# The branch over a general path: its wait, its hints and its flag, in a fused attention and token-mixing kernel

## The chip, the cores and the metric

The kernel runs on one core of a Trainium2 chip. The metric is the device time of one execution in microseconds (us). Before the change the median of three runs is 108.28 us (108.19 to 108.72). A program of this kind repeats to about 0.5%, or 0.54 us.

A core has five instruction streams that matter here: TensorE (PE; its weight loads are shown as PEld), VectorE (DVE), ScalarE (ACT), GpSimd (POOL) and SyncE (SP). A name with a q, such as DVEq, is the sequencer of that engine, which takes the instructions in program order, carries out waits, register loads and branches itself, and hands the rest to the engine. Stores to DRAM are issued by SP, loads by GpSimd; 16 DMA engines carry them, and they also carry the blocks of instructions that the sequencers ask for (the queues of kind "instruction").

## What is computed

For 4 batches, 8 heads, 768 rows and head size 64: five rounds of Sinkhorn normalisation of an 8x8 matrix for each head, a mix of the 8 blocks of K and V by it, attention within each block of 96 rows, and then a token mixer on the joined heads.

```python
P = sort_net
for _ in range(5):
    P = np.exp(P - np.max(P, axis=-1, keepdims=True))
    P = P / (np.sum(P, axis=-1, keepdims=True) + 1e-09)
    P = P / (np.sum(P, axis=-2, keepdims=True) + 1e-09)
k_sorted = np.einsum('bhij,bhjcd->bhicd', P, k_b)      # v_sorted likewise
scores = scale * np.matmul(q_b, k_sb.transpose(0, 1, 2, 4, 3))
scores = scores - np.max(scores, axis=-1, keepdims=True)
attn = np.exp(scores)
attn = attn / (np.sum(attn, axis=-1, keepdims=True) + 1e-09)
x = np.matmul(attn, v_sb)                              # heads joined: 4 x 768 x 512
W_tok = scale * np.einsum('bsd,btd->bst', x @ w_q, x @ w_k)
out = np.maximum(np.einsum('bst,btd->bsd', W_tok, x), 0.0) @ w_out
```

## The kernel before

The fast path leaves out the maximum of the scores. It takes the plain exponential and keeps the reciprocal of every row sum in `RS`. At the end a test on GpSimd (lines 465 to 472) counts the entries of `RS` that lie between 1e-30 and 1e30, and writes 1 to `bad` if any does not. `bad` is then loaded into a register of four engines (GpSimd, ScalarE, TensorE, VectorE; line 474), and under `tc.If(redo > 0)` (line 476) stands the general path: the whole computation once more, unrolled, with the maximum. With these inputs the flag is 0, and the engines jump over it. Its length is very different from engine to engine: on TensorE it holds thousands of matmuls, on ScalarE the 32 exponentials.

The fast path is unrolled too. The schedule is manual: the string `ORDER` (lines 18 to 51) is the program order, one item for each unit of work, and each engine takes its own items in that order. An item is a letter, the batch, an index, and after the @ a PSUM bank (for TensorE) or the engine. The items that matter here are those of the last batch, 3, at the end of the string:

- `G3.n` builds the small mixing matrix `Ab` from `wk` and `X` (8 matmuls), `g3.0` evacuates it.
- `H3.n` mixes the tokens, 4 matmuls into two banks; `h3.n` is the ReLU into `mixT`, for output rows 2n and 2n+1.
- `O3.n` is one output product (4 matmuls over `mixT` and `wo`; `O3.5` is split into halves a and b), and `o3.n` its evacuation into `ot`, by ScalarE (`@A`) or VectorE (`@D`).
- `y3.n` is the store of one sixth of the last batch, 256 KB, issued by SP (line 445). `ot` has four slots of two sixths each. The six last stores read three of them: slots 1, 2 and 3 hold the sixths 0 and 1, 2 and 3, 4 and 5.
- `P3.n` and `x3.n` are the attention product and its division; `x3.n` writes `RS`, and `x3.1` is the last to do so.

The end of the order before reads:

```python
y2.2@S o3.1@D O3.3@5 o3.0@D O3.4@0 y3.0@S o3.3@A y3.1@S O3.5a@1 y3.3@S o3.4@D O3.5b@7 o3.5a@A O3.2@6
y3.4@S o3.5b@A y3.5@S o3.2@A y3.2@S
```

So the last product is O3.2, the last evacuation o3.2 on ScalarE, and the last store y3.2. Waits follow from the tiles: an instruction that writes a tile waits until the earlier ones that read it are done, a store's landing included.

The branch of line 476 works so on each of the four engines: a first compare-and-branch on the flag, a semaphore instruction that makes up for the counts of the path that is left out, and, with `preferred_fallthrough_block=False`, a second branch to the end of the kernel. There (line 577) each engine runs a drain, SP walks over the semaphores of all queues and engines one by one, and a barrier ends the program.

Of the kernel before, what the change touches and what calls it, by code (L numbers as in the profile page):

```python
# [10 lines left out]
BF16 = mybir.dt.bfloat16  # L11
AX = mybir.AxisListType
ALU = mybir.AluOpType
# [26 lines left out]
P2.2@0 o0.1@A P2.3@4 o0.0@A x2.2@D O0.4@3 P2.0@6 o0.4@A x2.3@D S3.4@0 O0.5@2 e3.4@A x2.0@D H0.1@4  # L40
o0.5@A S3.1@0 T2.3@3 h0.1@A T2.2@2 t2.3@D T2.1@6 T2.0@7 t2.2@D P3.3@4 t2.1@D t2.0@A O0.2@3 x3.3@D
e3.1@A P3.4@6 J2.0@2 o0.2@A x3.4@D P3.0@0 j2.0@A H1.2@4 x3.0@D H1.0@6 W2.0@3 h1.2@A O0.3@2 w2.0@A
P3.2@0 h1.0@A J2.1@3 x3.2@D P3.1@4 j2.1@A O1.0@6 o0.3@A x3.1@D y0.1@S T3.3@7 d2.1@S O1.1@3 y0.2@S
y0.0@S T3.1@2 o1.1@A d2.0@S H1.1@0 t3.1@D W2.1@4 G2.0@5 w2.1@A h1.1@D t3.3@A G2.1@5 T3.0@4 O1.5@7
t3.0@D T3.2@3 o1.5@D O1.4@2 t3.2@A O1.2@4 g2.0@A o1.4@D J3.0@7 o1.0@D O1.3@5 y1.0@S j3.0@D J3.1@0
o1.3@A o1.2@A H2.0@2 j3.1@D W3.0@1 H2.1@6 y1.1@S H2.2@4 w3.0@D W3.1@0 h2.0@D G3.0@1 w3.1@A h2.1@A
G3.1@1 O2.0@0 d3.1@A d3.0@A O2.1@2 o2.0@D O2.3@3 h2.2@D o2.1@A O2.2@0 y2.0@S o2.3@A y1.2@S g3.0@A
O2.5@6 o2.2@A y2.1@S H3.0@4 o2.5@D H3.2@2 H3.1@0 h3.0@A O2.4@7 h3.1@A O3.1@6 o2.4@D h3.2@A O3.0@4
y2.2@S o3.1@D O3.3@5 o3.0@D O3.4@0 y3.0@S o3.3@A y3.1@S O3.5a@1 y3.3@S o3.4@D O3.5b@7 o3.5a@A O3.2@6
y3.4@S o3.5b@A y3.5@S o3.2@A y3.2@S  # L50
"""

UNIT = re.compile(r"([A-Za-z])(\d)\.(\w+?)@(\w)$")
# [3 lines left out]
def kernel(  # L57
# [11 lines left out]
    nc = tc.nc  # L69
    B, H, S, D = q.shape  # L70
    NB = sort_net.shape[-1]
    BLK = S // NB
# [13 lines left out]
    AG = 14  # L86
    NG = -(-NU // AG)
    LAST = B - 1
# [6 lines left out]
    sb = ctx.enter_context(tc.tile_pool(name="sb", bufs=1))  # L95
    psp = ctx.enter_context(tc.tile_pool(name="psp", bufs=1, space=bass.MemoryType.PSUM))

    def tiles(name, n, shape, dtype=BF16):
        return [sb.tile(shape, dtype, name=f"{name}{i}") for i in range(n)]

    PS = psp.tile([P, 8, 512], FP32, name="ps")
# [13 lines left out]
    E = tiles("E", 2, [BLK, NT, EW])  # L115
# [7 lines left out]
    NOT = 4  # L123
    ot = tiles("ot", NOT, [P, 2, DM], FP32)
    M = tiles("M", 2, [P, H, SP, NB])
    RS = sb.tile([BLK, B, NG, 2, AG // 2], FP32, name="RS")
    ok = sb.tile([BLK, B, NG * AG], BF16, name="ok")
# [6 lines left out]
    m_p = sb.tile([P, SP], BF16, name="m_p")  # L134
    gate = sb.tile([1, 1], BF16, name="gate")
    ok1 = sb.tile([1, 1], FP32, name="ok1")
    bad = sb.tile([1, 1], mybir.dt.int32, name="bad")
    fil = sb.tile([P, 512], BF16, name="fil")

# [8 lines left out]
    def mm(o, w, x, start=True, stop=True, t=False):  # L148
        nc.tensor.matmul(o, w, x, is_transpose=t, start=start, stop=stop, skip_group_check=True)  # L149
# [71 lines left out]
    def u_u(b, n, e, bank):  # L221
        copy(e, PTR.rearrange("p i h -> p (i h)"), PS[:, bank, 0:NB * (BH - H)])
# [211 lines left out]
    def oslot(b, n):  # L434
        return ot[(b * 3 + n // 2) % NOT][:, n % 2, :]
# [4 lines left out]
    def u_y(b, n, e):  # L440
# [3 lines left out]
        else:  # L444
            ENG[e].dma_start(out=od[:, n, :], in_=oslot(b, n))

    fns = {kk[2:]: f for kk, f in locals().items() if kk.startswith("u_")}
    halves = {"a": (0, DM // 2), "b": (DM // 2, DM)}
    banks = {}
    fills = dict(u="B", q="Q", k="K", v="V", f="F", e="S", x="P", t="T", j="J", w="W", g="G", h="H", o="O")  # L450
    for item in ORDER.split():
        kind, b, n, arg = UNIT.match(item).groups()
        b, half = int(b), halves.get(n[-1], ())
        num = int(n[:-1] if half else n)
        if kind in "BZQKVFSPTJWGHO":
            banks[kind, b, n] = int(arg)
            fns[kind](b, num, int(arg), *half)
        elif kind in fills:
            fns[kind](b, num, arg, banks[fills[kind], b, "1" if kind in "gu" else n], *half)
        else:  # L460
            fns[kind](b, num, arg)

    okf = ok.rearrange("p b n -> p (b n)")
    rsf = RS.rearrange("p b n a t -> p (b n a t)")
    ok2 = E[1][:, 0, 0:B * NG * AG]
    nc.gpsimd.tensor_scalar(out=okf, in0=rsf, scalar1=1e-30, scalar2=None, op0=ALU.is_ge)  # L468
    nc.gpsimd.tensor_scalar(out=ok2, in0=rsf, scalar1=1e30, scalar2=None, op0=ALU.is_le)
    nc.gpsimd.tensor_tensor(out=okf, in0=okf, in1=ok2, op=ALU.mult)  # L470
    nc.gpsimd.tensor_reduce(out=ok1, in_=okf, op=ALU.add, axis=AX.XYZWC)
    nc.gpsimd.tensor_scalar(out=bad, in0=ok1, scalar1=BLK * B * NG * AG - 0.5, scalar2=None, op0=ALU.is_lt)
    eng = mybir.EngineType
    redo = nc.values_load(bad, engines=(eng.Pool, eng.Activation, eng.PE, eng.DVE), min_val=0, max_val=1)

    with tc.If(redo > 0, preferred_fallthrough_block=False):
        qc = QT[1].rearrange("p k r s -> p k (r s)")
        sx = XT[1][0:BLK].rearrange("p t c -> p (t c)").bitcast(FP32)[:, 0:S]
        ex = E[1][:, 1, 0:S]
        exT = E[1][:, 2, 0:S]  # L480
        mx = RS.rearrange("p b n a t -> p (b n a t)")[:, 0:NB]
        sm = RS.rearrange("p b n a t -> p (b n a t)")[:, NB:2 * NB]

        def bb(t, w):
            return t.unsqueeze(2).to_broadcast([BLK, NB, w])

        spread(0, H, BH)
        u_u(0, 1, "D", 0)
        for b in range(B):
            for n in range(3):  # L490
                nc.gpsimd.dma_start(out=(Qn, Kn, Vn)[n][0].rearrange("p h r d -> p h (r d)"),
                                    in_=(q, k, v)[n][b].rearrange("h (p r) d -> p h (r d)", p=P))
            if b == 0:
                spread(1, 0, H)
                src = PS[:, 1, 0:NB * H].rearrange("p (i h) -> p h i", h=H)
            else:
                src = PTR.rearrange("p i h -> p h i")[:, (b - 1) * H:b * H, :]
            for n in range(NP):
                spread_m("D", 0, n, src)
            for n in range(NP):  # L500
                u_Q(0, n, 2)
                u_q(0, n, "D", 2)
                copy("D", qc[:, n].rearrange("p (i r s) -> p r i s", i=NB, r=R6),
                     QT[0][:, n].rearrange("p r (i s) -> p r i s", i=NB))
                u_K(0, n, 4)
                u_k(0, n, "D", 4)
                sorted_t(Vn, 0, n, 6)
                by_block("D", XT[0][:, n, :], 6)
                u_F(0, n, 3)
                u_f(0, n, "D", 3)  # L510
            for h in range(H):
                kp, o = h // 2, h % 2 * D
                sp = PS[0:BLK, 4:6, 0:4 * BLK].rearrange("p a (i c) -> p a i c", c=BLK)
                for i in range(NB):
                    mm(sp[:, i // 4, i % 4, :], qc[o:o + D, kp, i * BLK:(i + 1) * BLK],
                       KT[0][o:o + D, kp, i * BLK:(i + 1) * BLK])
                copy("D", sx.rearrange("p (a n) -> p a n", a=2), PS[0:BLK, 4:6, 0:4 * BLK])
                s3 = sx.rearrange("p (i c) -> p i c", i=NB)
                nc.vector.reduce_max(mx, s3, axis=AX.X)
                nc.vector.tensor_sub(s3, s3, bb(mx, BLK))  # L520
                nc.scalar.activation(ex, sx, ACT.Exp, scale=scale)
                nc.vector.reduce_sum(sm, ex.rearrange("p (i c) -> p i c", i=NB), axis=AX.X)
                nc.vector.reciprocal(sm, sm)
                for i in range(NB):
                    mm(bf(6)[0:BLK, i * BLK:(i + 1) * BLK], ex[:, i * BLK:(i + 1) * BLK],
                       idb[0:BLK, 0:BLK], t=True)
                copy("D", exT, bf(6)[0:BLK, 0:S])
                op = PS[0:BLK, 7, :].rearrange("p (i d) -> p i d", d=D)
                for i in range(NB):
                    mm(op[:, i, :], exT[:, i * BLK:(i + 1) * BLK], VT[0][:, i, h * D1:h * D1 + D])  # L530
                nc.vector.tensor_mul(X[0][:, kp, :, o:o + D], op, bb(sm, D))
            for n in range(PT):
                u_T(0, n, n % 2)
                u_t(0, n, "D", n % 2)
            for n in range(2):
                u_J(0, n, 2)
                u_j(0, n, "D", 2)
                u_d(0, n, "D")
                u_W(0, n, 3)
                u_w(0, n, "D", 3)  # L540
            for n in range(2):
                u_G(0, n, 2)
            u_g(0, 0, "D", 2)
            for n in range(3):
                u_H(0, n, 4)
                u_h(0, n, "D", 4)
            for n in range(R6):
                u_O(0, n, n % 2)
                u_o(b, n, "D", n % 2)
                if b == LAST or n % 2:  # L550
                    u_y(b, n if b == LAST else n // 2, "P")
# [30 lines left out]
```

## Time and profile before

The runs of before: 108.28 us in the median. The profiled execution took 108.6 us, of which the span of the profile is 106.8 us.

| | busy, us | share of the span |
|---|---|---|
| TensorE | 94.2 | 88% |
| VectorE | 74.1 | 69% |
| ScalarE | 69.9 | 65% |
| GpSimd | 31.3 | 29% |

The profile follows the chain that ended last back from the end; 80% of the span is TensorE in it. A line of the chain gives the start, the duration, engine, tile and source line. In a line of one source line's instructions stand the engine, the operation, the count, the duration in ns (least, median, most) and the first and last start in us. A line of DMA issues ends with the time from issue to landing, and a line of a DMA queue gives packets, MB and its share of the 16 engines. In the timeline the square brackets hold the idle time before an instruction, and what ended it.

### The profile page before, as it was taken

The page shows a single profiled execution, that of the slowest core. Times are in us where ns is not written, and L with a number is a line of the kernel's source. Part 1 is how long each engine was busy: PE and PEld are TensorE (multiplying, and loading weights), DVE is VectorE, ACT ScalarE, POOL GpSimd, SP SyncE. Part 2 cuts the span into 40 slices and gives each one's busy share as a digit, 9 for nine tenths or more (in the row PEclk, how much of TensorE's full clock was granted, in tenths as well). Part 3 has the DMA queues.
Part 4 walks back from the last instruction along what each step waited for, and adds up shares of the span by engine and source line. Part 5 has one row for each costly group of instructions (what it writes and reads, how often), then busy time and mean ns, then how long its engine had stood idle before and what let it go on. Part 6 is the DMA issues. An engine that isn't in the chain of part 4 may idle for free.

```text
span 106.8 us, 3637 instructions
## 1 busy us (share of the span) xinstructions
PE 94.2 (88%) x1556; PEld 65.7 (61%) x1556; DVE 74.1 (69%) x144; ACT 69.9 (65%) x101; POOL 31.3 (29%) x51
## 2 busy tenths in 40 slices
PE   5999989597698979889999999999999999999600
PEld 2334489486686966779868867597666565454300
DVE  2687689198797785788989977999767765455200
ACT  4101079769687879898879798688933448784400
POOL 5999089999229400000000000000077000000000
PEclk9999999999999999999999999999999999999975
DMA  0899999999999999999975373100059145496950
GB/s 3 91 201 205 203 203 210 200 203 205 205 204 204 188 202 211 198 203 208 205 161 159 94 211 96 44 6 0 6 196 388 45 196 203 160 408 236 381 196 18
DMA packets 18501, 18.57 MB, mean 174 GB/s; under 512 B 1840, under 2 KB 16560, under 8 KB 18480
## 3 DMA queue, kind: packets, MB, share of 16 engines
q0 software_dynamic: 14064, 10.09, 62.8%
q1 hardware_dynamic: 4416, 8.19, 22.0%
q8 instruction: 14, 0.23, 0.9%
q14 instruction: 7, 0.06, 0.1%
HBM read 20.19 MB, written 6.29 MB: 248 GB/s over the span
## 4 chain that ended last, share of the span: by engine, by line
PE 80%; ACT 6%; issue 4%; DVE 3%; DVEq 0%; ACTq 0%
PE ps L149 80%; ACT E L339 3%; DVE X L364 1%; ACT Vs L153 1%; DVE KT L155 1%; ACT XT L153 1%; ACT QT L153 1%; ACT ot L153 1%; DVE M L233 0%; DVE wk L155 0%; DVE fil L170 0%; DVE RS L362 0%; DVE Pm L169 0%; DVEq L155 0%; ACTq L153 0%
## 5 line engine op out<-in xcount | busy, mean ns | idle before, releaser
L339 ACT ACTIVATE E<-ps 96x960 bf16<-96x960 f32 (+1 forms) x28 | 24.6, 905 | 2.9 <-PE ps L149 2.6
L149 PE MATMUL ps<-wo,mixT 128*128 128x512 bf16 (+1 forms) x100 | 22.9, 371 | 0.0
L364 DVE TENSOR_TENSOR X<-ps,RS 96x896 bf16<-96x896 f32 (+1 forms) x20 | 20.1, 1007 | 0.7
L149 PEld LDWEIGHTS <-mixT 128*128 128x128 bf16 x100 | 8.9, 98 | 8.6 <-issue 0.2
L153 ACT COPY ot<-ps 128x512 f32<-128x512 f32 (+1 forms) x16 | 8.8, 560 | 8.1 <-PE ps L149 4.7
L468 POOL TENSOR_SCALAR ok<-RS 96x280 bf16<-96x280 f32 x1 | 0.9, 924 | 41.9 <-DVE RS L362 41.9
L149 PE MATMUL ps<-fil 128*128 128x512 bf16 x40 | 11.7, 466 | 1.2 <-DVE fil L170 1.2
L149 PE MATMUL ps<-VT,E 96*128 96x65 bf16 x256 | 11.2, 194 | 1.4 <-DVE X L364 0.8
L149 PEld LDWEIGHTS <-E 96*128 96x128 bf16 x256 | 9.8, 97 | 3.6 <-issue 1.5
L149 PE MATMUL ps<-QT,KT 64*128 64x96 bf16 x256 | 9.9, 204 | 1.6 <-issue 1.3
L233 POOL TENSOR_TENSOR M<-PTR,m_p 128x256 bf16<-128x256 bf16 x12 | 8.8, 750 | 7.4 <-PE ps L149 4.1
L155 DVE COPY ot<-ps 128x512 f32<-128x512 f32 x9 | 6.1, 691 | 6.1 <-PE ps L149 3.2
L149 PEld LDWEIGHTS <-fil 128*128 128x128 bf16 x40 | 4.5, 116 | 7.9 <-issue 3.8
L153 ACT CAST KT<-ps 128x768 bf16<-128x768 f32 x10 | 7.7, 805 | 2.0 <-PE ps L149 1.9
L149 PEld LDWEIGHTS <-KT 64*128 64x128 bf16 x256 | 6.8, 94 | 2.9 <-issue 1.6
L149 PE MATMUL ps<-idb,X 96*128 96x96 bf16 x128 | 7.5, 206 | 0.6 <-issue 0.6
L149 PE MATMUL ps<-M,Kn 128*64 128x128 bf16 x192 | 7.5, 221 | 0.3 <-issue 0.3
L155 DVE COPY QT<-ps 128x768 bf16<-128x768 bf16 x13 | 6.7, 551 | 1.4 <-PE ps L149 1.1
L425 ACT ACTIVATE mixT<-ps 128x1024 bf16<-128x1024 f32 x7 | 7.0, 1026 | 0.9 <-PE ps L149 0.6
L149 PEld LDWEIGHTS <-X 96*128 96x128 bf16 x128 | 6.2, 98 | 1.9 <-issue 0.9
L155 DVE COPY VT<-ps 96x1024 bf16<-96x1024 bf16 x7 | 4.8, 687 | 3.5 <-PE ps L149 2.7
L149 PE MATMUL ps<-idb,Qn 128*64 128x128 bf16 x192 | 7.0, 220 | 0.1
(78 smaller groups left out, 154.0 us busy)
## 6 DMA issues: line engine op xcount, KB each, us to landing
out_dram<-ot SPq DMA_DIRECT2D x9, 512.0 KB, 2.8
Kn<-in_k_dram POOLq DMA_DIRECT2D x4, 768.0 KB, 12.8
Vn<-in_v_dram POOLq DMA_DIRECT2D x4, 768.0 KB, 14.7
Qn<-in_q_dram POOLq DMA_DIRECT2D x4, 768.0 KB, 15.1
VT<-Vs SPq DMA_DIRECT2D x12, 130.0 KB, 2.5
out_dram<-ot SPq DMA_DIRECT2D x6, 256.0 KB, 2.7
wo<-in_moe_w_out_dram POOLq DMA_DIRECT2D x1, 512.0 KB, 22.7
qD<-qkT SPq DMA_DIRECT2D x6, 48.0 KB, 2.6
```

Source lines behind the costliest of these rows:

```text
L149: nc.tensor.matmul(o, w, x, is_transpose=t, start=start, stop=stop, skip_group_check=True)
L153: nc.scalar.copy(o, i)
L155: nc.vector.tensor_copy(o, i)
L233: ENG[e].tensor_tensor(out=M[b % 2][:, h0:h1], in0=src[:, h0:h1].unsqueeze(2).to_broadcast([P, 2, SP, NB]), in1=m_p.unsqueeze(1).unsqueeze ...
L339: nc.scalar.activation(E[b % 2][:, n, 0:2 * w * BLK].rearrange("p (t a c) -> p a t c", a=2, c=BLK), PS[0:BLK, bank:bank + 2, 0:w * BLK].re ...
L364: nc.vector.tensor_mul(xo.rearrange("p (a t d) -> p a t d", a=2, d=D), ps[:, :, :, 0:D], rs.unsqueeze(3).to_broadcast([BLK, 2, w, D]))
L425: nc.scalar.activation(o, i, ACT.Relu)
L468: nc.gpsimd.tensor_scalar(out=okf, in0=rsf, scalar1=1e-30, scalar2=None, op0=ALU.is_ge)
```

## The change

The test of the row sums becomes an item `test` of the order, behind `x3.1`. The load of the flag becomes an item `flag`, behind `o3.1@D` and ahead of `O3.3`. Two new items mark places for branch hints, "LikelyTaken" for the branch labelled `redo`: `hintT` for TensorE ahead of `G3.0`, `hintD` for VectorE ahead of `H3.0` (on VectorE's own stream, ahead of `o2.5`). Ahead of the `If` stand three memsets on VectorE, each of which writes one element of each half of a slot of `ot` and so waits for the stores from it, a memset of a new tile `past`, a 1x1 matmul and a ScalarE copy that read `past`. And the preferred fallthrough becomes the general path, so that going past it is the taken branch.

```diff
-O2.5@6 o2.2@A y2.1@S H3.0@4 o2.5@D H3.2@2 H3.1@0 h3.0@A O2.4@7 h3.1@A O3.1@6 o2.4@D h3.2@A O3.0@4
-y2.2@S o3.1@D O3.3@5 o3.0@D O3.4@0 y3.0@S o3.3@A y3.1@S O3.5a@1 y3.3@S o3.4@D O3.5b@7 o3.5a@A O3.2@6
-y3.4@S o3.5b@A y3.5@S o3.2@A y3.2@S
...
+P3.2@0 h1.0@A J2.1@3 x3.2@D P3.1@4 j2.1@A O1.0@6 o0.3@A x3.1@D test y0.1@S T3.3@7 d2.1@S O1.1@3
...
+J3.1@0 o1.3@A o1.2@A H2.0@2 j3.1@D W3.0@1 H2.1@6 y1.1@S H2.2@4 w3.0@D W3.1@0 h2.0@D hintT G3.0@1
+w3.1@A h2.1@A G3.1@1 O2.0@0 d3.1@A d3.0@A O2.1@2 o2.0@D O2.3@3 h2.2@D o2.1@A O2.2@0 y2.0@S o2.3@A
+y1.2@S g3.0@A O2.5@6 o2.2@A y2.1@S hintD H3.0@4 o2.5@D H3.2@2 H3.1@0 h3.0@A O2.4@7 h3.1@A O3.1@6
+o2.4@D h3.2@A O3.0@4 y2.2@S o3.1@D flag O3.3@5 o3.0@D O3.4@0 y3.0@S o3.3@A y3.1@S O3.5a@1 y3.3@S
+o3.4@D O3.5b@7 o3.5a@A O3.2@6 y3.4@S o3.5b@A y3.5@S o3.2@A y3.2@S
...
+    past = sb.tile([1, 4], BF16, name="past")
...
+    def test():
+        okf = ok.rearrange("p b n -> p (b n)")
+        rsf = RS.rearrange("p b n a t -> p (b n a t)")
+        ok2 = E[LAST % 2][:, 0, 0:B * NG * AG]
+        nc.gpsimd.tensor_scalar(out=okf, in0=rsf, scalar1=1e-30, scalar2=None, op0=ALU.is_ge)
...
+    def flag():
+        redo.append(nc.values_load(bad, engines=(eng.Pool, eng.Activation, eng.PE, eng.DVE), min_val=0, max_val=1))
+
+    def hint(e):
+        tc.mark_branch_hint_location("redo", "LikelyTaken", engines=(eng.PE if e == "T" else eng.DVE,))
...
-    redo = nc.values_load(bad, engines=(eng.Pool, eng.Activation, eng.PE, eng.DVE), min_val=0, max_val=1)
-
-    with tc.If(redo > 0, preferred_fallthrough_block=False):
+    for n in range(3):
+        nc.vector.memset(ot[(LAST * 3 + n) % NOT][0:1, :, 0:1], 0.0)
+    nc.vector.memset(past[:, 0:1], 0.0)
+    mm(PS[0:1, 0, 0:1], past[:, 0:1], past[:, 0:1])
+    nc.scalar.copy(past[:, 1:2], past[:, 0:1])
+    with tc.If(redo[0] > 0, preferred_fallthrough_block=True, label="redo"):
```

The five instructions of the test are the same as before, and the general path is unchanged.

More of the change, by code (lines that the diff above doesn't have):

```diff
@@ L42 @@
 e3.1@A P3.4@6 J2.0@2 o0.2@A x3.4@D P3.0@0 j2.0@A H1.2@4 x3.0@D H1.0@6 W2.0@3 h1.2@A O0.3@2 w2.0@A
[L43 to L47, printed above, removed]
-O2.5@6 o2.2@A y2.1@S H3.0@4 o2.5@D H3.2@2 H3.1@0 h3.0@A O2.4@7 h3.1@A O3.1@6 o2.4@D h3.2@A O3.0@4
-y2.2@S o3.1@D O3.3@5 o3.0@D O3.4@0 y3.0@S o3.3@A y3.1@S O3.5a@1 y3.3@S o3.4@D O3.5b@7 o3.5a@A O3.2@6
-y3.4@S o3.5b@A y3.5@S o3.2@A y3.2@S
+P3.2@0 h1.0@A J2.1@3 x3.2@D P3.1@4 j2.1@A O1.0@6 o0.3@A x3.1@D test y0.1@S T3.3@7 d2.1@S O1.1@3
+y0.2@S y0.0@S T3.1@2 o1.1@A d2.0@S H1.1@0 t3.1@D W2.1@4 G2.0@5 w2.1@A h1.1@D t3.3@A G2.1@5 T3.0@4
+O1.5@7 t3.0@D T3.2@3 o1.5@D O1.4@2 t3.2@A O1.2@4 g2.0@A o1.4@D J3.0@7 o1.0@D O1.3@5 y1.0@S j3.0@D
+J3.1@0 o1.3@A o1.2@A H2.0@2 j3.1@D W3.0@1 H2.1@6 y1.1@S H2.2@4 w3.0@D W3.1@0 h2.0@D hintT G3.0@1
[3 more added lines that the diff above has]
+o3.4@D O3.5b@7 o3.5a@A O3.2@6 y3.4@S o3.5b@A y3.5@S o3.2@A y3.2@S
 """
@@ L445, in u_y @@
             ENG[e].dma_start(out=od[:, n, :], in_=oslot(b, n))
+    eng = mybir.EngineType
+    redo = []
+    def test():
[3 more added lines that the diff above has]
+        nc.gpsimd.tensor_scalar(out=okf, in0=rsf, scalar1=1e-30, scalar2=None, op0=ALU.is_ge)
+        nc.gpsimd.tensor_scalar(out=ok2, in0=rsf, scalar1=1e30, scalar2=None, op0=ALU.is_le)
+        nc.gpsimd.tensor_tensor(out=okf, in0=okf, in1=ok2, op=ALU.mult)
+        nc.gpsimd.tensor_reduce(out=ok1, in_=okf, op=ALU.add, axis=AX.XYZWC)
+        nc.gpsimd.tensor_scalar(out=bad, in0=ok1, scalar1=BLK * B * NG * AG - 0.5, scalar2=None, op0=ALU.is_lt)
+    def flag():
+        redo.append(nc.values_load(bad, engines=(eng.Pool, eng.Activation, eng.PE, eng.DVE), min_val=0, max_val=1))
+    def hint(e):
+        tc.mark_branch_hint_location("redo", "LikelyTaken", engines=(eng.PE if e == "T" else eng.DVE,))
     fns = {kk[2:]: f for kk, f in locals().items() if kk.startswith("u_")}
@@ L451 @@
     for item in ORDER.split():
+        if item in ("test", "flag"):
+            (test if item == "test" else flag)()
+            continue
+        if item.startswith("hint"):
+            hint(item[-1])
+            continue
         kind, b, n, arg = UNIT.match(item).groups()
@@ L461 @@
             fns[kind](b, num, arg)
[L465 to L476, printed above, removed]
+    for n in range(3):
[4 more added lines that the diff above has]
+    with tc.If(redo[0] > 0, preferred_fallthrough_block=True, label="redo"):
         qc = QT[1].rearrange("p k r s -> p k (r s)")
```

## The prediction, made before the changed kernel was run

> **What bounds the kernel now.** I read the page first, then the chain of waits, then the end of the timeline, then single lines of the code in short windows. Times are us from the start of the span.
>
> ```profile
> span 106.8 us, 3637 instructions
> q8 instruction: 14, 0.23, 0.9%
> q14 instruction: 7, 0.06, 0.1%
> ...
> 62.66 37.81 PE ps L149 x435
> 100.49 0.59 ACT ot L153
> ...
> 101.10 0.33 SPq L445 DMA_DIRECT2D out_dram<-ot  x1
> ...
> SPq L577 <- DMA out_dram<-ot: 3.8, 2, 2.5
> ```
>
> TensorE carries the chain from 62.66 to 100.47, ScalarE evacuates the last product until 101.08, and SP issues the last store at 101.10. The span goes on for 5.7 us with no compute in it. In the waits of SP's own queue, 3.8 us of this are waits for stores to land. So the stage to look at is the tail. The stores issued in it, in order of their issue, each in its own window (the last column is from issue to landing):
>
> ```profile
> out_dram<-ot SPq DMA_DIRECT2D x1, 256.0 KB, 2.0
> out_dram<-ot SPq DMA_DIRECT2D x2, 256.0 KB, 2.2
> out_dram<-ot SPq DMA_DIRECT2D x2, 256.0 KB, 2.4
> out_dram<-ot SPq DMA_DIRECT2D x1, 256.0 KB, 2.8
> out_dram<-ot SPq DMA_DIRECT2D x1, 256.0 KB, 4.2
> out_dram<-ot SPq DMA_DIRECT2D x1, 256.0 KB, 4.4
> ```
>
> The first took 2.0; the backlog brings that to 2.8 for the fourth; then it jumps to 4.2 and 4.4, though no more stores follow. (The windows overlap, so two rows count two stores.) The last lands at 101.1 + 4.4 = 105.5. What changed is seen in the transfers by queue in two windows, 102.3 to 103.05 and 103.05 to 105.1:
>
> ```profile
> q1 hardware_dynamic: 99, 0.17, 63.2%
> q8 instruction: 1, 0.02, 10.7%
> q14 instruction: 2, 0.02, 6.0%
> ...
> q1 hardware_dynamic: 18, 0.03, 8.9%
> ```
>
> Queues q8 and q14 carry instructions: 0.23 MB in 14 packets is 16 KB each, 0.06 MB in 7 is 8 KB. Three such blocks arrive amid the last stores. By 103.05 all store packets but 18 have moved; these 18, 0.03 MB, dribble on until 105. Nearly all of the 256 KB was out two us before the landing, and the rest sat behind something on a few of the 16 DMA engines. I read it as the instruction blocks. Who asked for them:
>
> ```profile
> L474 PEldq TENSOR_LOAD <-bad x1: 744/744/744, 97.3 to 97.3; - x1
> L474 DVEq TENSOR_LOAD <-bad x1: 986/986/986, 98.8 to 98.8; - x1
> L474 ACTq TENSOR_LOAD <-bad x1: 738/738/738, 100.5 to 100.5; - x1
> ...
> L476 ACTq COMPARE_BRANCH  x2: 38/42/45, 101.3 to 101.5; - x2
> L476 DVEq COMPARE_BRANCH  x1: 51/51/51, 100.5 to 100.5; - x1
> L476 PEldq COMPARE_BRANCH  x1: 4413/4413/4413, 100.6 to 100.6; - x1
> ...
> L577 ACTq DRAIN  x1: 66/66/66, 101.9 to 101.9; - x1
> L577 SPq EVENT_SEMAPHORE  x7: 28/28/28, 105.5 to 105.9; - x7
> L577 SPq DRAIN  x2: 7/7/7, 106.0 to 106.0; - x2
> L577 PEldq DRAIN  x1: 72/72/72, 105.1 to 105.1; - x1
> L577 DVEq DRAIN  x1: 63/63/63, 105.5 to 105.5; - x1
> ```
>
> TensorE's second branch, over the general path, takes 4.4 us (100.6 to 105.1). VectorE branches at 100.5 and does its next instruction at 105.5: 5.0 us. ScalarE, whose general path is short, is through 0.4 us after its second branch (101.5 to 101.9). So two engines jump far and wait for code, and their fetches and the last stores hold each other up. SP passes the last landing at 105.5, walks seven semaphores by 106.0, and the closing barrier takes 0.8 more, to 106.8.
>
> **The change part by part**, against the profiled span of 106.8. That execution took 108.6 in all, 1.8 outside the span, and is 0.3 above the median of 108.28; I take the gain off the median.
>
> *The test of the row sums moves into the order, after x3.1.* It waits for the last of the row sums either way, and it is on GpSimd, which idles; nothing is queued behind it that anyone needs. GpSimd's own branches are 22 us before the end:
>
> ```profile
> L476 POOLq COMPARE_BRANCH  x2: 38/39/40, 83.8 to 84.7; - x2
> ```
>
> Cost 0.
>
> *The flag's loads move ahead of O3.3, on TensorE, VectorE and ScalarE.* On TensorE 744 ns on the sequencer, with O3.3 behind it. Its cover is the queue of dispatched matmuls: the load stood at 97.3 above, while the products that were already dispatched ran until 100.47, so the sequencer had 3.2 us in hand.
>
> ```profile
> 93.90 2.85 ACT L425 ACTIVATE mixT<-ps 128x1024 bf16<-128x1024 f32 x3 [0.61 <-PE ps L149]
> ...
> 94.23 4.06 PE L149 MATMUL ps<-wo,mixT 128*128 128x512 bf16 x18
> ...
> 96.17 0.69 DVE L155 COPY ot<-ps 128x512 f32<-128x512 f32 x1 [0.17 <-PE ps L149]
> 97.10 0.69 DVE L155 COPY ot<-ps 128x512 f32<-128x512 f32 x1 [0.24 <-PE ps L149]
> 98.81 0.69 DVE L155 COPY ot<-ps 128x512 f32<-128x512 f32 x1 [1.02 <-PE ps L149]
> 97.94 0.59 ACT L153 COPY ot<-ps 128x512 f32<-128x512 f32 x1 [1.18 <-issue]
> ```
>
> At the new place it is released when the first of the three mixT groups is out (93.90 + 2.85/3 = 94.85). Eight matmuls at some 0.22 us (4.06/18) then stand ahead of O3.3: 1.8 us of cover for 0.74. Cost 0; without cover, 0.7. On VectorE 986 ns falls between the copies at 96.17 and 97.10: o3.0 slips by about 0.1 us and the copy at 98.81, which has a wait of 1.02 before it, not at all; the slip delays one early store, cost 0. On ScalarE the 738 ns lie in the idle 1.18 before 97.94. Their old places at the tail come free: ScalarE's first branch at 101.3 had waited for the load of 100.5, though nothing waited for it. Gain 0.
>
> *The two hints.* One instruction on TensorE ahead of G3.0, one on VectorE ahead of o2.5:
>
> ```profile
> 87.95 1.15 PE L149 MATMUL ps<-X,wk 96*64 96x256 bf16 x16
> 93.63 0.69 DVE L155 COPY ot<-ps 128x512 f32<-128x512 f32 x1 [1.63 <-ACT ot L153]
> ```
>
> The trace has no hint. Nearest rows: a branch, 51 ns on VectorE. I take 0, bounds 0 to 0.1 us each; VectorE idles 1.6 us near it. If a hint fetches a block at once, one of 16 engines is held for about 1 us (10.7% of 16 engines in 0.75 us is 1.3) in a stretch with 8 us left to recover.
>
> *The wait.* Three memsets on VectorE write into each of the three slots of ot that the six last stores read, so each waits until its two stores have landed; a fourth writes `past`; a 1x1 matmul on TensorE and a copy on ScalarE read `past`. Behind these stand the branches of all three engines, and behind them the closing barrier. Nobody else waits. GpSimd and SP are not held. What it buys: no branch is taken, and no far code asked for, before the last store has landed. The last store then lands as the undisturbed engines did: the packets of 103.05 and about 0.25 for the semaphore, 103.3, or 2.2 after its issue (bounds 2.0 and 2.8 from the rows above: 103.1 to 103.9). Against 105.5: minus 2.2.
>
> ```profile
> L169 DVE MEMSET Pm<- x1: 65/65/65, 0.8 to 0.8; 32x8 f32 x1
> ...
> L153 ACT COPY ot<-ps 128x256 f32<-128x256 f32 x2 | 0.7, 373 | 0.7 <-PE ps L149 0.7
> L149 PE MATMUL ps<-VT,E 96*128 96x65 bf16 x256 | 11.2, 194 | 1.4 <-DVE X L364 0.8 <-issue 0.6
> ```
>
> After the landing: the slot of O3.2's store is the second of the three, so two slot memsets and that of `past` remain, 3 x 65 ns and gaps, 0.3 us (bounds 0.2 to 0.6). Then the matmul (below 194 ns) beside ScalarE's copy (below 373 ns): 0.25 (0.1 to 0.45). Then the branch with code at hand, as ScalarE's from 101.3 to its drain at 101.9: 0.6 (0.3 to 0.8). SP's walk over the semaphores runs beside these. Then the drain and barrier as before, 0.85. Sum: 103.3 + 0.3 + 0.25 + 0.6 + 0.85 = 105.3, a gain of 1.5 on 106.8. The stall goes to the same landing as before, only an earlier one, and the branch behind it is now serial.
>
> *The fallthrough turned round* makes the way past the general path the branch that is taken, which the hint names. Before, the skipping engine fell through and then jumped; one jump takes the place of the other, counted in the 0.6.
>
> **Rivals.**
>
> A, the hints do not bring the code. Then TensorE and VectorE miss as before, but only after the landing, where nothing hides it: place, the branch at about 103.9; price, the fetch. Bounds: its packet alone, 1.2, and VectorE's 5.0. The 4.4 and 5.0 had the stores in their way; with an empty queue I take 2.8. It decides from 1.5 us of exposed fetch on. Time 106.8 + 2.8 = 109.6 (108.0 to 111.8), slower. For it: nothing in this trace shows a hint at work, and both far jumps missed. Against: the hints stand 16 and 10 us ahead of the branch, a multiple of a fetch.
>
> [...]
>
> B, the hints work, but a block still meets the last stores: VectorE has more instructions at its end than before, and one 8 KB block (q14) entering between 99 and 103 us holds one DMA engine. Price: the landing goes from 2.2 to the 2.8 of the backlogged store, 0.6. Time 107.4. For it: instruction blocks do arrive in this stretch above. Against: they came from the branches.
>
> C, VectorE's hint is in time only in part (its block is asked for when the sequencer enters the last stretch, while the stores drain): half the fetch of A is exposed, 1.4. Time 108.2 (107.8 to 108.8), no change. Against it: 3 us of wait for the last store is enough for most fetches.
>
> **How the numbers follow.** Forecast 0.52 (its own range 106.3 to 107.2, from a landing at 103.1 or 103.5 and the bounds of the steps behind it); B 0.18; C 0.11; A 0.16; better still, 106.0 or less, 0.03. Time 106.8. The range 106.0 to 109.0 leaves out 0.03 below and most of A, 0.1, above. Faster by over 0.5% (about what a measurement of this kernel tells from no change; 107.74): 0.71, the forecast, the better case and nearly all of B. Within 0.5%: 0.13, C and a little of B. Slower (over 108.82): 0.16, A.
>
> **What would show it.** The last store should land 2.0 to 2.8 after its issue at about 101.1; no far-jump branch over 0.5 us on TensorE or VectorE; the instruction blocks of q8 and q14 absent between 101 and 103, and one more of each earlier; the memset group at 103.3; the copies and matmuls up to 101.1 unmoved. A branch of TensorE of over 1 us after the landing makes the forecast wrong by rival A; a landing at 103.9 or later, by B.

## The result, and the profile after

The changed kernel takes 107.75 us (8 runs, 107.41 to 107.97), the kernel before, measured beside it, 108.31 us. The ratio is 0.9945, with a 95% interval of 0.9926 to 0.9964: 0.56 us faster. The prediction had 106.8, so a gain of 1.5; a little over a third of it came. Times here and below are medians of runs in the chip's fast state; one run of e8, at 111.24, was in the slow one and is not counted.

The page of the changed kernel, and the issue of its first and of its last store of batch 3, each in a window of its own (the last column is from issue to landing):

```profile
span 106.1 us, 3639 instructions
q8 instruction: 13, 0.21, 0.8%
q14 instruction: 6, 0.05, 0.1%
...
out_dram<-ot SPq DMA_DIRECT2D x1, 256.0 KB, 2.1
...
out_dram<-ot SPq DMA_DIRECT2D x1, 256.0 KB, 2.9
```

The last store lands 2.9 us after its issue. Before it took 4.4, and the prediction had 2.2. Its issue has hardly moved (101.14 against 101.10). The chain of waits of the changed kernel, its last steps (the view leaves out the shortest pieces):

```profile
100.52 0.59 ACT ot L154
101.14 2.92 DMA out_dram<-ot
104.20 0.07 issue
104.26 0.06 DVE ot L493
104.33 0.07 issue
104.39 0.06 DVE ot L493
104.52 0.19 ACT past L496
```

So the landing is at 104.06 (101.14 + 2.92), and 2.0 us stand behind it up to the end at 106.1, as many as the prediction had in sum. The branches and the drains, as lines of the code:

```profile
L497 DVEq COMPARE_BRANCH  x1: 84/84/84, 104.4 to 104.4; - x1
L497 ACTq COMPARE_BRANCH  x1: 45/45/45, 104.5 to 104.5; - x1
L497 PEldq COMPARE_BRANCH  x1: 397/397/397, 104.5 to 104.5; - x1
...
L598 ACTq DRAIN  x1: 8/8/8, 105.1 to 105.1; - x1
L598 DVEq DRAIN  x1: 17/17/17, 105.1 to 105.1; - x1
L598 PEldq DRAIN  x1: 8/8/8, 105.1 to 105.1; - x1
...
L598 DVEq BRANCH_PREFETCH_HINT  x1: 51/51/51, 0.8 to 0.8; - x1
L598 PEldq BRANCH_PREFETCH_HINT  x1: 50/50/50, 0.8 to 0.8; - x1
```

The jumps are short now. TensorE's takes 0.4 us in place of 4.4, and VectorE is at its drain 0.7 us after its branch in place of 5.0. (The 4.4 and the 5.0 ran beside the last stores; in e4 below, without the hints and with all stores landed, they are 3.5 and some 3.4.) The last two rows hold a surprise: both hints run at 0.8 us, at the very start, and not where the marks stand in the order.

What is left over is 0.7 us of landing. Two views point at it. In the transfers between 100.2 and 102 there is one instruction packet, a block of 8 KB (6 packets of q14 are 0.05 MB), amid the last stores; and on VectorE the copy of o3.4 starts at 99.22, with 1.40 of idle time before it, where the kernel before had 98.81 and 1.02:

```profile
q14 instruction: 1, 0.01, 1.1%
...
97.13 0.69 DVE L156 COPY ot<-ps 128x512 f32<-128x512 f32 x1 [0.24 <-PE ps L150]
99.22 0.69 DVE L156 COPY ot<-ps 128x512 f32<-128x512 f32 x1 [1.40 <-PE ps L150]
```

The theory from this, T1: VectorE crosses into a new block of instructions at this copy, the 192nd of its records, stalls 0.4 us there (1.40 against 1.02), and the block that it then asks for holds one DMA engine while the last stores drain. The rival, T2: the stores' own backlog makes 2.9.

### The profile page after: what moved, and what is told of

It is laid out like the page before. It is cut to its first block, busy times and chain, and to the rows that moved or that the text cites. A ratio compares the mean times of both kernels' runs of the same rounds, so it can differ in the third digit from the quotient of the medians.

```text
span 106.1 us, 3639 instructions
## 1 busy us (share of the span) xinstructions
PE 93.6 (88%) x1550; PEld 65.7 (62%) x1557; DVE 74.3 (70%) x148; ACT 70.1 (66%) x102; POOL 31.2 (29%) x51
## 4 chain that ended last, share of the span: by engine, by line
PE 80%; ACT 6%; issue 5%; DVE 3%; DMA 3%; DVEq 0%; ACTq 0%
PE ps L150 80%; ACT E L340 3%; DMA out_dram<-ot 3%; DVE X L365 1%; ACT Vs L154 1%; DVE KT L156 1%; ACT XT L154 1%; ACT QT L154 1%; ACT ot L154 1%; DVE M L234 0%; DVE wk L156 0%; DVE fil L171 0%; DVE RS L363 0%; ACT past L496 0%; DVE ot L493 0%
## 5 line engine op out<-in xcount | busy, mean ns | idle before, releaser
L150 PE MATMUL ps<-wo,mixT 128*128 128x512 bf16 (+1 forms) x93 | 22.2, 370 | 0.5 <-issue 0.2
L154 ACT COPY XT<-ps 128x768 bf16<-128x768 bf16 x6 | 4.8, 798 | 3.6 <-PE ps L150 3.6
```

Of the source, the lines that this page charges most:

```text
L154: nc.scalar.copy(o, i)
```

## The experiments

Everything up to the last store shifts as a whole from one profiled execution to the next (VectorE's last three copies start at 96.17, 97.10 and 98.81 in the kernel before and at 95.92, 96.85 and 98.57 in e1), so the spans of single profiles differ by some tenths for no reason in the tail. The time from the issue of the last store to its landing is free of this, and the medians average over it.

| kernel | time, us | ratio to before (95%) | last store, issue to landing |
|---|---|---|---|
| the change | 107.75 | 0.9945 (0.9926 to 0.9964) | 2.9 |
| e1, 12 memsets earlier on VectorE | 106.89 | 0.9881 (0.9864 to 0.9898) | 2.2 |
| e2, 2 memsets earlier on VectorE | 106.92 | 0.9873 (0.9857 to 0.9888) | 2.2 |
| e9, flag behind o3.4 | 107.65 | 0.9947 (0.9931 to 0.9963) | 2.9 |
| e3, no wait | 107.79 | 0.9943 (0.9919 to 0.9966) | 4.0 |
| e5, e1 without the wait | 107.59 | 0.9934 (0.9913 to 0.9955) | 3.1 |
| e4, no hints | 110.96 | 1.0237 (1.0214 to 1.0259) | 2.9 |
| e8, e1 without VectorE's hint | 109.46 | 1.0113 (1.0075 to 1.0151) | 2.2 |
| e10, before with the wait alone | 111.64 | 1.0313 (1.0292 to 1.0334) | 3.0 |
| e7, e1 with the late flag | 107.52 | 0.9921 (0.9898 to 0.9943) | 2.2 |
| e6, e1 with the slots in another order | 106.54 | 0.9853 (0.9832 to 0.9874) | 2.2 |

### e1: move VectorE's crossing away from the stores

```diff
+    def pad(n):
+        for _ in range(n):
+            nc.vector.memset(past[:, 2:3], 0.0)
...
-y1.2@S g3.0@A O2.5@6 o2.2@A y2.1@S hintD H3.0@4 o2.5@D
+y1.2@S g3.0@A O2.5@6 o2.2@A y2.1@S hintD pad12 H3.0@4 o2.5@D
```

> The changed kernel with 12 one-element memsets on VectorE ahead of o2.5, where VectorE idles. Theory T1: the last store of the changed kernel lands 2.9 us after its issue because VectorE enters a new 128-instruction block at the copy of o3.4 (0.4 us of stall) and the 8 KB for it (queue q14, 100.8) holds one DMA engine while the last stores drain. With 12 more instructions it enters that block at about 92, when no store is near its end: the copy of o3.4 is back at 98.8, no instruction packet between 95 and 104, the last store lands 2.1 to 2.3 after its issue, span 105.3, time 107.0. Theory T2: the landing is the backlog of the stores themselves: landing still 2.7 to 3.0 after the issue, span 106.1, time 107.8.

The time is 106.89. In the profile of e1, the instruction packet between 91 and 93; then VectorE's timeline; then the last store:

```profile
q14 instruction: 1, 0.01, 1.0%
...
91.69 1.36 DVE L471 MEMSET past<- 1x1 bf16 x12
...
98.57 0.69 DVE L156 COPY ot<-ps 128x512 f32<-128x512 f32 x1 [1.02 <-PE ps L150]
...
out_dram<-ot SPq DMA_DIRECT2D x1, 256.0 KB, 2.2
```

The block has moved to 91.6 by twelve instructions that do nothing (between 95 and 104 this profile has no instruction packet), the copy of o3.4 has its old idle time of 1.02, and the last store lands after 2.2, the figure of the forecast. T2 is out. That 12 memsets, 1.36 us in all, move the block from 100.8 to 91.6 also speaks for the count of instructions as what places it.

### e2 and e9: the block, or the slip of o3.4?

e1 removes both the block amid the stores and the stall at o3.4, which delays two stores by 0.4 us. e2 has 2 memsets in place of 12, so that the crossing falls into a wait of VectorE.

> The changed kernel with 2 such memsets. The new block is then entered at a wait of VectorE at about 97.2, so the copy of o3.4 is on time (98.8), but the 8 KB still come amid the stores, at about 98.5 to 99. T1a, the block on the DMA engine makes the landing late: still 2.7 to 2.9 after the issue, time 107.6 to 107.8. T1b, the 0.4 us by which o3.4 and its two stores slip makes it late: landing 2.2, time 107.0 to 107.1.

The time is 106.92, and the last store lands after 2.2: what T1b expected. But the profile of e2 shows why this doesn't decide. In the window from 98 to 99, the first row has the busy share of the DMA engines in 40 slices of 25 ns:

```profile
DMA  9498881000900000000000000029049969948968
...
q14 instruction: 1, 0.01, 2.8%
```

The block (the lone 9 in the middle of the noughts, at 98.25; the view books a packet in the slice in which it starts) fell into a gap between the stores. Beside it the slices are empty, and over the whole microsecond the store queue had 46.7% of the engines. So e9 leaves the pads out and moves the flag's load behind o3.4. The crossing then comes one instruction later, the copy is on time, and the block comes where it came in the changed kernel.

```diff
-o2.4@D h3.2@A O3.0@4 y2.2@S o3.1@D flag O3.3@5 o3.0@D O3.4@0 y3.0@S o3.3@A y3.1@S O3.5a@1 y3.3@S
-o3.4@D O3.5b@7 o3.5a@A O3.2@6 y3.4@S o3.5b@A y3.5@S o3.2@A y3.2@S
+o2.4@D h3.2@A O3.0@4 y2.2@S o3.1@D O3.3@5 o3.0@D O3.4@0 y3.0@S o3.3@A y3.1@S O3.5a@1 y3.3@S
+o3.4@D flag O3.5b@7 o3.5a@A O3.2@6 y3.4@S o3.5b@A y3.5@S o3.2@A y3.2@S
```

> The changed kernel, no pads, with the flag's load behind o3.4 instead of ahead of O3.3. VectorE then enters its last block one instruction later, at the flag's load, so the copy of o3.4 and its two stores are on time (0.4 us earlier than in the changed kernel), and the 8 KB block still comes at about 100.9, amid the last stores. T1a, the block on the DMA engine makes the landing late: 2.8 to 3.0 after the issue, time 107.7. T1b, the slip of o3.4 made it late: landing 2.2, time 107.0.

The profile of e9, between 100.2 and 102, on VectorE and for the last store:

```profile
q14 instruction: 1, 0.01, 1.1%
...
98.56 0.69 DVE L156 COPY ot<-ps 128x512 f32<-128x512 f32 x1 [1.02 <-PE ps L150]
...
out_dram<-ot SPq DMA_DIRECT2D x1, 256.0 KB, 2.9
```

With the copy on time and the block in the stream of stores, the landing is 2.9 and the time 107.65, that of the changed kernel. So T1a holds: the block, not the slip, makes the landing late, and of these runs only where the stores fill the engines (the store queue at 100.9% of them around the block in the changed kernel, 102.7% in e9; in e2's gap the landing stays at 2.2).

### e3 and e5: what the wait buys

e3 leaves the four memsets, the matmul and the copy ahead of the branch out; the hints, the early flag and the fallthrough stay.

> The changed kernel without the four memsets, the matmul and the copy ahead of the branch; the hints, the early flag and the fallthrough stay. If the wait is what protects the stores: each engine enters the target block before the last store has landed, and the next sequential blocks (16 KB for TensorE, 8 KB for VectorE and ScalarE, seen at 105.6 in the changed kernel) arrive between 99 and 102.5; landing 3.0 to 4.4 after the issue (104.2 to 105.5), and 1.3 behind it: span 105.5 to 106.8, time 107.3 to 108.6. If the hints alone remove the traffic: landing as in the changed kernel (104.05), but only 1.3 behind it and not 2.0: span 105.35, time 107.1.

The time is 107.79, the same as with the wait. The profile of e3 between 97.5 and 103, and its last store:

```profile
q8 instruction: 1, 0.02, 1.4%
q14 instruction: 2, 0.02, 0.7%
...
out_dram<-ot SPq DMA_DIRECT2D x1, 256.0 KB, 4.0
```

The engines jump early, three blocks arrive in this stretch, a fourth follows at 103.5, still ahead of the landing, and the landing takes 4.0. What the wait saves there it costs behind the landing: 2.0 us to the end in place of 1.3. The same with the crossing moved away:

> e1 without the wait (no memsets on the slots, no matmul, no copy ahead of the branch), hints and pads kept. If the wait earns something once the early block is out of the way: the blocks behind the targets (16 KB for TensorE at 98.2, 8 KB at about 101.9 and 103.5 as in e3) still meet the stores, the last store lands 3.0 to 4.0 after its issue, 1.3 behind it, span 105.1 to 106.1 against 105.1 of e1, time 107.0 to 107.9. If it earns nothing: landing 2.2 to 2.5 and 1.3 behind it, span 104.4 to 104.7, time 106.2 to 106.5.

107.59 against 106.89 of e1, with a landing of 3.1. Between 97.5 and 103 three blocks arrive here too. Once the early block is gone, the wait is worth 0.7 us; without that, nothing.

The two runs show one thing more. VectorE's branch and its next instruction, in e3 and then in e5:

```profile
L492 DVEq COMPARE_BRANCH  x1: 84/84/84, 99.0 to 99.0; - x1
L492 DVEq EVENT_SEMAPHORE  x1: 21/21/21, 101.8 to 101.8; - x1
...
L499 DVEq COMPARE_BRANCH  x1: 84/84/84, 98.6 to 98.6; - x1
L499 DVEq EVENT_SEMAPHORE  x1: 21/21/21, 99.3 to 99.3; - x1
```

In e3 VectorE's instructions up to the copy of o3.4 are those of the changed kernel, so it branches right behind its crossing, and although it has its hint it is held for 2.8 us (99.0 to 101.8). In e5 the pads have put the crossing some 7 us ahead of the branch (91.6 in e1, 98.6), and the same jump takes 0.7.

### e4, e8 and e10: what the hints buy

e4 is the changed kernel without its two hints.

> The changed kernel without the two hints. If the hints bring the target block: TensorE and VectorE miss at the branch behind the landing, 1.2 to 5.0 us, my guess 2.8: span 108.9, time 110.6, slower than before. If they do nothing and the branch hits for another reason: as the changed kernel, 107.75.

110.96, slower than before by 2.4%. The branches of e4:

```profile
L497 DVEq COMPARE_BRANCH  x1: 72/72/72, 104.6 to 104.6; - x1
L497 PEldq COMPARE_BRANCH  x1: 3495/3495/3495, 104.8 to 104.8; - x1
...
L598 DVEq DRAIN  x1: 17/17/17, 108.1 to 108.1; - x1
```

TensorE misses for 3.5 us and VectorE for some 3.4, with all stores landed. e8 takes VectorE's hint alone out of e1:

> e1 without VectorE's hint; TensorE's stays. If each hint covers its own engine's miss: VectorE takes 3.0 to 3.4 us from its branch to its drain, as in e4, TensorE 0.4; span 108.0, time 109.8. If one fetch serves both or only TensorE's was needed: as e1, 106.9.

109.46. The branches and VectorE's drain in e8, and its packet between 91 and 92:

```profile
L504 DVEq COMPARE_BRANCH  x1: 72/72/72, 103.4 to 103.4; - x1
L504 PEldq COMPARE_BRANCH  x1: 402/402/402, 103.5 to 103.5; - x1
...
L605 DVEq DRAIN  x1: 17/17/17, 106.7 to 106.7; - x1
...
q14 instruction: 1, 0.01, 3.8%
```

TensorE, with its hint, jumps in 0.4; VectorE, without, takes 3.3 us to its drain. So TensorE's hint did nothing for VectorE, which with its own took 0.7 (the changed kernel). One block of q14 comes in this stretch in e1 and in e8 alike (at 91.6 and 91.4), with and without VectorE's hint.

e10 is the kernel before with the wait's six instructions alone.

> The kernel before with the wait alone: the four memsets, the matmul and the copy ahead of its branch, no hints, the flag and the fallthrough as before. TensorE and VectorE miss behind the landing, as in e4 (3.4 to 3.5 us from branch to drain), and VectorE's 8 KB block still comes at about 100.9: landing 2.9, span 109.3, time 111.0. If the fallthrough as before saves the jump: 108.3.

111.64: the misses behind the landing, and 0.5 us that e7 explains. The transfers of e10 from 101.4 to 102.3, and then from 102.3 to 103.05, where the kernel before had three instruction packets:

```profile
q1 hardware_dynamic: 190, 0.33, 102.2%
q14 instruction: 1, 0.01, 2.1%
...
q1 hardware_dynamic: 107, 0.19, 67.2%
```

The three are gone, as the wait was meant to bring about. One block is left, although no engine of e10 but GpSimd has branched yet, and the last store lands after 3.0.

### e7: the early flag

```diff
-o2.4@D h3.2@A O3.0@4 y2.2@S o3.1@D flag O3.3@5 o3.0@D
+o2.4@D h3.2@A O3.0@4 y2.2@S o3.1@D O3.3@5 o3.0@D
...
+    flag()
     for n in range(3):
         nc.vector.memset(ot[(LAST * 3 + n) % NOT][0:1, :, 0:1], 0.0)
```

> e1 with the load of the flag back behind the whole order, ahead of the slot memsets. If the early flag is worth nothing, as the prediction costs it (the loads of 0.5 to 0.8 us end by 101.3, long before the landing at 103.1): as e1, 106.9. If the early place costs or saves something: more than 0.2 us away from e1.

107.52, 0.6 us above e1 (0.4 by the ratios): the expectation that it costs nothing fell. The loads of the flag in e7:

```profile
L464 DVEq TENSOR_LOAD <-bad x1: 970/970/970, 98.9 to 98.9; - x1
L464 ACTq TENSOR_LOAD <-bad x1: 738/738/738, 100.5 to 100.5; - x1
L464 PEldq TENSOR_LOAD <-bad x1: 492/492/492, 103.8 to 103.8; - x1
```

VectorE and ScalarE load before the landing. TensorE loads at 103.8, behind it:

```profile
103.82 0.07 PEld L150 LDWEIGHTS <-past 1*1 1x1 bf16 x1 [3.84 <-DVE past L502]
104.33 0.16 PE L150 MATMUL ps<-past 1*1 1x1 bf16 x1 [3.85 <-DVEq L505]
```

The weight load of `past`, which waits for the landing, starts together with the flag's load, and the matmul only behind it. From this I read that TensorE's stream has the weight load ahead of the flag's load, against the order of the source. The 0.5 us are then serial.

### e6: a faster version

The slot of the last store, O3.2's, is the second of the three memsets. With the order 0, 2, 1 it comes last, and one memset fewer, with its wait, stands behind the landing.

```diff
-    for n in range(3):
+    for n in (0, 2, 1):
         nc.vector.memset(ot[(LAST * 3 + n) % NOT][0:1, :, 0:1], 0.0)
```

> e1 with the slot memsets in the order 0, 2, 1, so that the slot of the last store comes last and only that memset and the one of past stand behind the landing. The changed kernel spends 0.13 us on the memset of slot 3 and its wait between. Expected: 0.13 to 0.2 us less than e1, time 106.7, span 104.9. If the branch and not the memsets sets the tail: as e1, 106.9.

106.54, or 0.9853 of the kernel before: the best of the study, and 1.2 us below the changed kernel (1.0 by the ratios), in two edits (12 idle memsets and the order of three others). Its interval (0.9832 to 0.9874) overlaps a little with that of e1, so the 0.3 us between these two is less sure than the rest.

## Why the prediction was right and wrong

**The bottleneck and the mechanism: right.** The tail behind the last issue, the far jumps of TensorE and VectorE, and the instruction blocks that meet the last stores were the things to look at, and the change acts on them. Without hints and wait, both engines miss and the landing is 4.4; with both it is 2.9 and the jumps are 0.4.

**The step that failed** is in the part on the wait: "The last store then lands as the undisturbed engines did ... 103.3, or 2.2 after its issue". It landed 2.9 after its issue, and 0.7 of the forecast gain of 1.5 went there. The step took every instruction block near the last stores for one of the branches, and so for gone. The three blocks between 102.3 and 103.05 on which it rests were of the branches: e10 has none of them. But a fourth stands just ahead of that window. The transfers of the kernel before from 101.4 to 102.3:

```profile
q14 instruction: 1, 0.01, 2.2%
```

e10 still has it. With this one block the landing is 3.0, so of the 2.2 us between 4.4 and 2.2 the branches' blocks were 1.4 and this one 0.8. I take it for VectorE's: it comes with VectorE's branch behind it in time (e10) as with it ahead (before), and 12 more instructions on VectorE take it to 91.6. e1 moves this crossing and gives the landing of 2.2 and, with 106.89, the time that the forecast named. Rival B described just this, with its place, its cause and its size (8 KB, one DMA engine, 0.6 us, a landing of 2.8, 107.4), and got a chance of 0.18 with the argument "they came from the branches". The trace of before could have corrected that by the block at 101.7, and by the branches of TensorE and of VectorE in it:

```profile
L476 PEldq COMPARE_BRANCH  x2: 95/2254/4413, 98.1 to 100.6; - x2
L476 DVEq COMPARE_BRANCH  x2: 51/53/55, 100.3 to 100.5; - x2
```

TensorE's first branch follows its flag's load within 0.1 us (97.3 + 0.74 = 98.0). VectorE's stands 0.5 us behind the end of its own (98.8 + 0.99 = 99.8). I read this as the crossing, and the block at 101.7 as its fetch. Rival B's own reason, that VectorE has more instructions at its end than before, is not needed: the kernel before has the block too.

No row shows the 0.25 us that the same step puts between the last packet and the landing; in e1 the last packet of the stores starts by 102.65, and the memset that waits for the last store starts at 103.26. With the 0.2 from landing to memset of the changed kernel (104.06 to 104.26) the landing is at 103.06, about 0.4 behind the packet: an estimate.

**The steps behind the landing: right in sum, in part by luck.** From the landing at 104.06 VectorE's branch comes after 0.4 us (forecast 0.3), its drain after another 0.7 (0.6), the end 1.0 later (0.85). The matmul and the copy, forecast at 0.25, add nothing: ScalarE's copy of `past` starts at 104.52, and its branch, in the sequencer, at 104.5 beside it.

**The hints: right in their work, wrong in their place and their fetches.** I had them ahead of G3.0 and o2.5, at 88 and 93.6, and "one more" block of each queue earlier. They run at 0.8 us, far ahead of their marks, and there is no additional block: 13 packets in q8 and 6 in q14, where before had 14 and 7.

**Rival A's mechanism is real, its condition false.** Its price was put at 2.8 and is 3.4 to 3.5 us (e4). Without its hint TensorE's jump took 3.5 us (e4), with it 0.4 (the changed kernel, and e8).

**Rival C's mechanism is real too, and the wait hides it.** In e3, with the branch right behind the crossing, VectorE is held for 2.8 us in spite of its hint. In the changed kernel the crossing (99.2) is 5 us ahead of the branch (104.4), and nothing of it shows.

**The flag: half right.** At its new place nothing is seen of it, as worked out: the last copy starts at 100.52, against 100.49 before. But "gain 0" held only against the kernel before, whose load stands ahead of any wait; together with the wait it is worth 0.4 to 0.6 us (e7).

**The size, in all**: 0.7 us of landing, which e1 gives back, is the miss in the profile. The medians add a little: before lay 0.3 below its profiled execution, the changed kernel 0.2.

## What to carry to other kernels

Where a program ends with stores and a branch over long code, look for instruction packets among the last stores: an 8 KB block there cost 0.7 us of landing here (2.9 against 2.2), as much as an evacuation (0.69), and one came with no branch of TensorE, VectorE or ScalarE ahead of it (e10). Count all blocks in that stretch, and tell for each who asked for it. Twelve idle instructions on that engine, placed where it waits anyway, moved the fetch out of the way here (100.8 to 91.6). The wait that was meant to protect the stores was worth 0.7 us once no other block met them (e1 against e5), and nothing while one did (the changed kernel against e3); and what stands behind such a wait, a flag's load included (0.49 us in e7), is on the path.

## What the hardware showed that was not expected

- The packets of q8 are 16 KB (0.21 MB in 13), those of q14 8 KB (0.05 MB in 6). Two instructions of VectorE start some 0.4 us late in the kernel before, 128 apart in its records: the 64th, a reciprocal at 27.4 (1.06 of idle time ahead of it, against 0.67 for the same one in the changed kernel), and the 192nd, the branch at 100.3. In the changed kernel the 192nd is the copy of o3.4, with 1.40 of idle time in place of 1.02. My reading is that VectorE crosses into a new block every 128 instructions; e1, in which 12 more of them move the block of q14 from 100.8 to 91.6, agrees.
- With a block in a stretch in which the stores keep the DMA engines busy (100.9% in the changed kernel, 102.7% in e9), the last landing came 2.9 after its issue, and 2.2 with the block elsewhere (e1), though its own packet takes about 0.3 (1.1% of 16 engines in 1.8 us); why it costs twice its own time stays open. In a gap between stores it cost nothing (2.2 in e2).
- A hint whose record stands at 0.8 us still served a branch at 104.5 (0.4 us on TensorE, 3.5 without it in e4), over 3,000 instructions later there (1550 matmuls and 1557 weight loads in the page of the changed kernel).
- VectorE, with its hint, was held for 2.8 us in e3, where the branch follows the crossing at once, and for 0.7 in e5, where the crossing lay some 7 us ahead.
